# Ordering the first loads of a hand-scheduled attention + MLP kernel, with a new table of priorities

## The chip, the cores and the metric

The kernel runs on one core of a Trainium2 chip. The metric is device time in microseconds (us) of one execution; lower is better. The profiled execution has a "span", from its first to its last instruction, which is some 1.7 us shorter than the time of the same run. Engines: PE (TensorE, matrix products), ACT (ScalarE), DVE (VectorE), POOL (GpSimd), and SP, the engine that issues the DMAs here.

On one core, a run counts as slow when it is over 1.5% above the fastest run of the same kernel.

## The reference

One layer norm feeds two branches whose outputs are added to the input:

```python
xn  = layernorm(x)                           # x: 2048 x 512
out = x + attention(xn) + silu(xn @ w1) @ w2 # w1: 512 x 1792
# attention: 32 heads of 16, 4 segments of 512 rows; in each segment
#   local part : softmax(q k^T / 4 + causal mask) v
#   memory part: phi(q) M / (phi(q) z), with M, z summed over earlier segments
#   o = g * memory + (1 - g) * local,  g = sigmoid(beta), one gate per head
#   the result is o @ wo
```

All tensors are bf16. Two details matter. The scores cannot start before q and k exist, and the fixed order of both kernels begins with the k and q products, so wk and wq are needed first. And `beta`, 32 numbers, is needed only when local and memory parts are weighted, much later.

## The kernel before

A planner in Python runs when the kernel is built. It makes a list of operations, each with an engine, an estimated duration and dependencies, and lays them out greedily: at each step every engine picks, among its operations that could start first, the one with the lowest `due`. The result is a fixed instruction order for each engine. `due` comes from `PRIO`, a table of 1,064 numbers found by an offline search against the planner's own estimate.

```python
def op(...):                            # cut to one line
    o.due = int(PRIO[unit] if PRIO else due)

def load(keys, fn, due, lat, nb=0):     # a DMA issue on SP; lat: estimated time to landing
    return op("SP", 520, lat, fn, due, w=keys, kind="load", not_before=nb)

load([("x", 0, 0)], ld_x(0, 0), 0, 2300)        # operation 0
load([("x", 0, 1)], ld_x(0, 1), 1, 2900)        # 1
load([("wk",)], ld_w("wk", "A_wk"), 2, 4200)    # 2
load([("wq",)], ld_w("wq", "A_wq"), 3, 5000)    # 3
load([("wv",)], ld_w("wv", "A_wv"), 4, 6900)    # 4
load([("w1",)], ld_w("w1", "B_w1"), 5, 11500)   # 5
load([("x", 1, 0)], ld_x(1, 0), 6, 12000)       # 6
load([("x", 1, 1)], ld_x(1, 1), 7, 12500)       # 7
load([("w2",)], ld_w("w2", "B_w2"), 8, 17000)   # 8
load([("wo",)], ld_w("wo", "A_wo"), 9, 18000)   # 9
op("SP", 1600, 2300, beta, 30000, w=[("bcol",)], kind="load", not_before=14000)  # 10: three small DMAs
# ... (cut) loads of x for segments 2 and 3, not before 26000 ns
```

The estimates of landing, `lat`, rise in the order of the list, but each stays with its load wherever the load is placed. The planner doesn't know that loads share one queue. With `PRIO`, the due time written in the list is ignored, and the old table put wk seventh and wq ninth.

```python
key, _, t, o = min(
    (
        -(10**9) if o.kind == "S" else -(10**8) if o.kind == "PV" and after_s else o.due,
        o.n, t, o,
    )
    for t, o in cands if t <= tmin + {"S": SLACK_S, "exp": 200}.get(o.kind, 0)
)
```

"S" are the score products (q k^T) into `psS`, a single PSUM buffer. Each of the 80 is read by one big exponential on ACT (128 x 2048, 1.88 us), so scores and exponentials alternate. The user of `beta` is the gate, on ACT and POOL; it stands among the exponentials:

```python
def gate(K):
    for n, c, sc in ((64, 0, -0.5), (16, 1, -0.5), (P, 2, 0.5)):
        g = K.gcol[0:n, c : c + 1]
        K.nc.scalar.activation(out=g, in_=K.bcol[0:n, c : c + 1], func=AF.Tanh, scale=sc)
        K.nc.gpsimd.tensor_scalar(
            out=g, in0=g, scalar1=1.0, scalar2=0.0, op0=ALU.add, op1=ALU.add
        )
op("ACT", 700, 400, gate, 36000, r=[("bcol",)], w=[("gcol",)])
```

The softmax here doesn't subtract the row's maximum and nothing guards it: scores larger than these inputs give would overflow.

Of the kernel before, what the change touches and what calls it, by code (L numbers as in the profile page):

```python
# [16 lines left out]
S = 2048  # L17
# [17 lines left out]
SLACK_S = 140  # L35
# [47 lines left out]
class Op:  # L83
# [7 lines left out]
    -223886, -213142, 63705, 177752, 22538, 11838, 1323, -178954, 67144, 313387, 373006, -21515,  # L91
    -130461, -113893, -392237, -225704, -39247, 247190, 57588, 37283, 207192, -218991, 308507,
    -194611, -201621, 108204, 211932, 13621, 191955, -74326, -130154, -216427, 359611, -155119,
    211539, -11405, 331460, -686597, 105504, -573941, 130428, -187273, 363457, -85128, 26133,
    606903, -210234, -48374, -297013, 60798, -86752, 132802, 118851, -12546, 272870, -132982, 56639,
    276934, -30169, -123830, -33891, 174675, 348195, 23174, 311678, 85348, -120105, 131741, -343655,
    153058, 64242, -128605, 30195, 365519, 429917, 204159, 219852, 21171, 419872, 463879, -39762,
    -46133, -123987, 230528, 410142, 339477, 252091, -376123, -41682, 194296, 83947, -35832,
    -276286, 321232, -145594, -524228, -181427, -294070, 301993, 29359, -431758, -6753, -615407,
    130942, -456522, 728205, -128974, -538322, -36195, 368831, 324874, -212795, 3954, 24792, -96637,  # L100
    135035, 97677, 219505, 275780, 142732, -348149, -42889, 172395, 167352, 445291, -66175, -102014,
    -372410, 37471, 173532, 19691, -321703, -129398, 162590, 242096, 70777, 150541, -390982, -61352,
    -251857, -193457, 59903, -1614, 300474, 282740, 64973, 208882, 311930, -142375, -31593, -66521,
    -186886, 104021, 173402, -103896, -310717, 19751, 214713, 406435, 162192, -59093, 104904, 15373,
    45642, -403821, 22920, -13329, -380672, -322525, -303614, -46256, 222990, 291846, 12582, 267990,
    156615, 34382, -299125, 93507, 42449, 95428, -70203, -72443, 71244, 84531, 355865, 214206,
    -51920, -867600, 450492, 653865, -124671, 291884, 109183, 371865, 49608, -24648, 12887, -52544,
    -107952, -196109, 126671, 210183, -73712, 65341, 327031, -272143, -81544, 72729, -135801,
    -44066, 81811, 504708, 242995, 322335, -108412, -218919, -420413, -151337, -268135, -61088,
    268203, -550455, 477679, 162280, 41945, 309807, 448567, -47735, 200, 219528, 257937, 308851,  # L110
    -4743, -77883, -321233, 271147, -158470, 70467, 161654, 183567, 109398, -58824, -26320, 319089,
    493049, -52901, -178879, -318844, -4681, 117496, -14816, -838748, -2790, -229724, 28284,
    -189806, 89509, -447653, -277801, 127390, -244192, 475390, 349318, -116303, 280396, -285555,
    297487, 646605, 233173, -505163, -444113, 544129, -247005, 360900, -207069, -518091, -25000,
    323687, 213790, 324998, 112059, -81929, 274310, -115137, -12298, -189996, 159842, -413389,
    43372, -6542, -361722, -117190, -181623, -209128, -95238, 561466, 65715, -562084, -398228,
    117345, 279724, -310824, 398752, 938804, 77902, -125744, -459583, -384468, 26680, 561173,
    156446, -76157, 212032, -558595, 670013, 310578, 166237, -657264, 247523, -22846, 83566, 303142,
    -142496, 182886, 339220, 121663, -215925, 16861, 413809, 204410, 470135, 547364, -35878, 56737,
    252649, 486999, 381304, 384370, 425566, -354622, -51398, 196368, -161285, -109610, 560866,  # L120
    582723, -347380, -50235, 665289, -31010, 302067, 262506, -423589, -284834, -306774, 300711,
    -55492, 364398, 189503, 404079, 265748, 536775, 393349, -113863, 795645, -43828, 650707, 144536,
    868479, 516187, -336929, 318957, -92765, -338554, 352320, 422504, 56954, -123776, 108661,
    -418893, 98624, -349798, 208932, -144548, 8421, 233612, 65865, 326473, 284664, -67576, 96797,
    54991, -86892, 225526, 106850, 145126, 120193, 89893, 406763, 9214, 938427, 229693, -8110,
    616416, 103328, 601485, -144743, -67828, 740495, -200273, 291414, 748381, 56526, 92062, 345312,
    27253, -319794, 121568, 100442, 437124, 302161, 427765, 119763, 54441, 335976, 297665, 714657,
    41060, 793859, -259467, -129865, 308076, 498970, 681180, 116086, -225150, 378154, 415845,
    349221, 140566, 644683, -124115, 173680, 11971, 399022, 400290, 655824, 224582, 305365, 700076,
    625561, 187056, -525661, 616109, -2218, -22419, -99519, -92630, -166436, -392391, 93383,  # L130
    -460739, 172173, 238659, -372180, 188021, 230765, 371908, 47890, -6346, 8122, -144220, 249370,
    617233, 40145, -137502, 166780, 97040, -40096, 58727, -276233, -226357, 345646, 181978, -46103,
    772501, 365050, -148600, -36316, 267507, 127581, -38572, 142382, -52113, 575324, -222372,
    -268435, 26343, 529066, 40508, 373069, 429467, 79014, 440198, 315329, 86662, -41603, 237281,
    476327, 356731, -99018, 265712, -249558, -49914, 4028, 301058, 592205, 470876, 154418, 96955,
    485673, -2411, 14098, 13735, 316163, -318442, 413197, -129226, 109000, -116788, 219469, 153645,
    47167, 518007, 183833, -30350, 699233, 211894, 322323, 263597, 83130, -227535, 236095, -85087,
    -113604, 37411, 430015, -2870, -5612, 278579, -362276, -83264, -81427, -199134, 58995, 569470,
    -109610, 201191, -659359, -190562, -403082, 227854, 631137, 226817, 48231, 419085, 98761,
    -79066, 216112, -643907, -35621, 508726, 32353, 93064, 164762, -316492, 382792, -92758, -169368,  # L140
    455126, -39072, 6864, -316685, 131619, 348879, 834577, -178579, 74157, -506959, 182481, 63075,
    -21058, 299346, 172655, -386925, -24498, -548053, 207605, 558009, -93423, -118774, -237046,
    217183, 552102, 680873, 306408, 531969, 445316, 434638, -200823, -13485, 118730, 20688, 107964,
    112865, 757871, -432568, -10969, 19072, 150683, 254327, 496949, -352315, 24731, -389605, -3730,
    320564, 957932, 373690, -57423, 83479, 690429, -376908, 253627, -914692, -30234, 29173, 73881,
    -206246, 230654, 445275, -30519, -472093, 309832, -118161, 1178607, 215829, -9127, 648306,
    427924, 332526, -202779, -136804, 21232, 611557, -135946, -198518, -226779, 238655, 259659,
    -193804, -267942, 238993, 81582, 270060, 107098, -115249, 474096, 12986, -18534, -216434,
    150625, 374025, 342160, 549418, 222611, 495391, 828493, 146361, 96622, 298454, -480090, 158394,
    -392573, 149486, 186067, -119362, 376881, -43805, -127619, -11352, -248776, -165409, 209429,  # L150
    917995, 102430, -131646, 202189, -151133, -397805, 219744, 242953, 155680, 79047, -1170477,
    7101, -3583, -372569, 484448, -160719, -239932, -484839, 5499, 210265, 306700, 256289, -348081,
    139835, 163395, -104101, 211338, 49815, 269523, 204999, 433551, 475223, -16588, 383302, -108148,
    165310, 444383, 89977, -44060, 198590, -369426, 249196, -37350, -199335, 220214, 431056, 529697,
    312339, 733114, -486947, 332194, 49609, 161813, -175730, -107076, 781937, 10229, 298989, 241713,
    110416, -111509, 121768, 243442, -152232, 353584, -245133, 182974, 37534, -157385, 569856,
    -260196, -545047, 254985, 138018, 20910, 66379, 21009, -656458, 367115, 483729, 180777, 19163,
    63118, 192957, 16971, -1949, 656916, 237358, 13970, 54310, 627127, 376175, -1475, 286123,
    312388, 30189, -484848, 289293, 961495, -115477, -152898, 258396, 175375, -401170, 350145,
    357588, 267082, -43812, -65319, -21881, 740140, 161674, 554201, 409656, 296631, 98022, 463505,  # L160
    248165, 41143, -45415, 310094, -120290, -92558, 132597, -2791, 43260, -488909, 468646, 750003,
# [24 lines left out]
class Plan:  # L186
# [763 lines left out]
    def schedule(self):  # L950
# [12 lines left out]
        mode, after_s, pend = "F", False, 0  # L963
# [194 lines left out]
```

## Time and profile before

| quantity | before | view |
|---|---|---|
| time, first three runs | 257.59 us (255.35 to 258.34) | runs |
| span of the profiled run | 253.2 us | page |
| PE / ACT busy | 89% / 77% | page, part 1 |
| first scores / first big exponential | 24.54 / 25.20 us | timeline |
| PE busy from 24.5 to 232 us | 195 of 207.5 us | stages |

The order of the loads is read from the timeline of SP. The columns are the start in us, the duration in us, the engine's queue, the line and the operation with what it writes and reads. `w` stands for w1 at the first place and w2 at the second.

```profile
0.79 1.99 SPq L296 DMA_DIRECT2D x_all<-in_A_x_dram  x4
2.82 0.47 SPq L304 DMA_DIRECT2D w<-in_B_w_dram  x1
3.33 0.51 SPq L304 DMA_DIRECT2D wv<-in_A_wv_dram  x1
3.88 0.51 SPq L304 DMA_DIRECT2D wk<-in_A_wk_dram  x1
4.43 2.68 SPq L304 DMA_DIRECT2D w<-in_B_w_dram  x1
7.16 6.01 SPq L304 DMA_DIRECT2D wq<-in_A_wq_dram  x1
13.21 1.88 SPq L304 DMA_DIRECT2D wo<-in_A_wo_dram  x1
```

The issue of wq lasts 6.01 us against about 0.5 for the first ones. I read this as the queue in front of it being full; no view shows the queue itself. What the late loads do to the PE is in its timeline; the bracket gives the idle time before an instruction and what ended it.

```profile
14.23 0.61 PE L276 MATMUL psb__201<-xnT__88,wk 128*128 128x512 bf16 x1 [4.47 <-DMA wk<-in_A_wk_dram]
...
21.01 1.89 PE L276 MATMUL psb__202<-xnT__88,wq 128*128 128x512 bf16 x4 [4.90 <-DMA wq<-in_A_wq_dram]
...
24.54 0.61 PE L609 MATMUL psS<-qT__102,kTo__96 32*128 32x512 bf16 x4
```

The first k product waits for wk until 14.23 us and the first q product for wq until 21.01 us. The layer norm had been done at 10.5 us (last cast into xnT, DVE timeline). The chain of waits that ended last, in order of time (start, duration, what), says the same for the whole execution:

```profile
4.43 2.68 SPq L304
...
7.16 13.81 DMA wq<-in_A_wq_dram
...
21.01 1.89 PE psb__202 L276 x4
```

The view by stages gives for each stretch its length and the busy time of each engine with the number of instructions, then the granted PE clock (1.00 is full), the DMA share and GB/s:

```profile
core 0: us, PE busy (x) PEld busy (x) DVE busy (x) ACT busy (x) POOL busy (x), PEclk, DMA share, GB/s
...
10.50:24.50 14.00, 5.16 (x11) 1.47 (x12) 1.38 (x2) 0.63 (x1) 1.27 (x2) 0.55 0.87 278
24.50:45.00 20.50, 18.80 (x119) 7.19 (x124) 17.92 (x36) 17.76 (x20) 16.75 (x40) 0.98 0.28 65
```

In the 14 us before the scores begin the PE works 5.16 us, at about half its clock. After that it is dense.

### The profile page before, as it was taken

The numbers are of one execution on the slowest core, as the hardware profiler recorded it, in microseconds if no ns is written. First come the engines' busy times: TensorE is split into PE (matmuls) and PEld (weight loads), VectorE is DVE, ScalarE is ACT, GpSimd is POOL, SyncE is SP. The second block draws the span as 40 slices with busy tenths as digits, with TensorE's granted clock in tenths as the row PEclk, the third lists the DMA queues.
The fourth block names the chain that finished last, engine by engine and source line by source line (L and its number), as shares of the span: only waits on it lengthen the run. The fifth ranks groups of instructions, "written<-read, shape, count | busy, mean of one in ns | idle before, by whom it ended". The sixth has DMA issues, their size and how long they took to land.

```text
span 253.2 us, 5054 instructions
## 1 busy us (share of the span) xinstructions
PE 224.4 (89%) x1887; PEld 96.9 (38%) x1920; DVE 178.2 (70%) x308; ACT 194.5 (77%) x170; POOL 130.0 (51%) x231
## 2 busy tenths in 40 slices
PE   7226997989999899999999998897999999997994
PEld 7102332443344343353443433342343434343441
DVE  4612988988758997688747799868676896366532
ACT  2100997998999989999899898997989887996000
POOL 4420996776769743358752447694833443432000
PEclk9955999999999999999999999999999999999999
DMA  6994125210322103214210221220101202201202
GB/s 204 385 349 142 22 41 146 25 31 14 63 52 45 23 18 121 64 43 108 51 34 10 86 71 31 68 66 12 56 22 54 70 14 89 73 4 36 76 22 83
DMA packets 29344, 18.52 MB, mean 73 GB/s; under 512 B 15752, under 2 KB 28808, under 8 KB 29320
## 3 DMA queue, kind: packets, MB, share of 16 engines
q1 hardware_dynamic: 29176, 18.07, 25.1%
q8 instruction: 15, 0.25, 0.5%
q10 hardware_dynamic: 144, 0.13, 0.2%
q14 instruction: 9, 0.07, 0.1%
HBM read 11.53 MB, written 2.33 MB: 55 GB/s over the span
## 4 chain that ended last, share of the span: by engine, by line
PE 38%; ACT 16%; DVE 16%; POOL 9%; DMA 9%; issue 6%; SPq 3%; DVEq 0%; ACTq 0%; POOLq 0%
PE psb__201 L276 6%; PE psb__204 L276 6%; PE psb__202 L276 6%; DMA wq<-in_A_wq_dram 5%; PE psb__203 L276 5%; PE psS L609 5%; ACT Pt__133 L620 2%; ACT Pt__129 L620 2%; ACT Pt__131 L620 2%; PE psO__2920 L929 2%; PE psO__2921 L929 2%; PE psO__2918 L929 2%; PE psO__2919 L929 2%; SPq L304 2%; ACT Pt__130 L620 2%
## 5 line engine op out<-in xcount | busy, mean ns | idle before, releaser
L276 PEld LDWEIGHTS <-w 128*128 128x128 bf16 x224 | 20.4, 98 | 26.3 <-issue 6.6
L620 ACT ACTIVATE Pt__128<-psS 128x2048 bf16<-128x2048 f32 x10 | 18.8, 1879 | 9.2 <-PE psS L609 8.7
L620 ACT ACTIVATE Pt__129<-psS 128x2048 bf16<-128x2048 f32 x10 | 18.8, 1878 | 2.9 <-PE psS L609 2.6
L620 ACT ACTIVATE Pt__130<-psS 128x2048 bf16<-128x2048 f32 x10 | 18.8, 1877 | 1.8 <-PE psS L609 1.5
L620 ACT ACTIVATE Pt__132<-psS 128x2048 bf16<-128x2048 f32 x10 | 18.8, 1878 | 1.8 <-PE psS L609 1.6
L620 ACT ACTIVATE Pt__135<-psS 128x2048 bf16<-128x2048 f32 x10 | 18.8, 1876 | 1.5 <-PE psS L609 1.2
L620 ACT ACTIVATE Pt__133<-psS 128x2048 bf16<-128x2048 f32 x10 | 18.8, 1878 | 1.5 <-PE psS L609 1.2
L620 ACT ACTIVATE Pt__134<-psS 128x2048 bf16<-128x2048 f32 x10 | 18.8, 1878 | 1.5 <-PE psS L609 1.3
L620 ACT ACTIVATE Pt__131<-psS 128x2048 bf16<-128x2048 f32 x10 | 18.8, 1879 | 1.0 <-PE psS L609 0.8
L634 POOL TENSOR_SCALAR_AFFINE_SELECT Pt__134<-Pt__134 128x512 bf16<-128x512 bf16 (+1 forms) x14 | 10.4, 756 | 10.0 <-ACT Pt__134 L620 9.9
L634 POOL TENSOR_SCALAR_AFFINE_SELECT Pt__133<-Pt__133 128x512 bf16<-128x512 bf16 (+1 forms) x15 | 10.2, 695 | 9.0 <-ACT Pt__133 L620 9.0
L634 POOL TENSOR_SCALAR_AFFINE_SELECT Pt__130<-Pt__130 128x512 bf16<-128x512 bf16 (+1 forms) x14 | 10.1, 738 | 9.1 <-ACT Pt__130 L620 9.1
L634 POOL TENSOR_SCALAR_AFFINE_SELECT Pt__135<-Pt__135 128x512 bf16<-128x512 bf16 (+1 forms) x14 | 9.2, 671 | 10.7 <-ACT Pt__135 L620 10.7
L634 POOL TENSOR_SCALAR_AFFINE_SELECT Pt__129<-Pt__129 128x512 bf16<-128x512 bf16 (+1 forms) x14 | 9.7, 707 | 9.3 <-ACT Pt__129 L620 9.3
L634 POOL TENSOR_SCALAR_AFFINE_SELECT Pt__128<-Pt__128 128x512 bf16<-128x512 bf16 (+1 forms) x14 | 10.2, 740 | 8.3 <-ACT Pt__128 L620 8.3
L634 POOL TENSOR_SCALAR_AFFINE_SELECT Pt__131<-Pt__131 128x512 bf16<-128x512 bf16 (+1 forms) x14 | 10.2, 742 | 7.5 <-ACT Pt__131 L620 7.5
L634 POOL TENSOR_SCALAR_AFFINE_SELECT Pt__132<-Pt__132 128x512 bf16<-128x512 bf16 (+1 forms) x13 | 10.1, 791 | 6.9 <-ACT Pt__132 L620 6.7
L276 PE MATMUL psb__201<-xnT__89,w 128*128 128x512 bf16 x44 | 11.7, 380 | 0.1
L276 PEld LDWEIGHTS <-wk 128*128 128x128 bf16 x64 | 6.3, 103 | 12.9 <-DMA wk<-in_A_wk_dram 4.6
L276 PE MATMUL psb__203<-xnT__88,w 128*128 128x512 bf16 x32 | 8.9, 379 | 2.5 <-DVE hT__140 L570 1.5
L276 PEld LDWEIGHTS <-wq 128*128 128x128 bf16 x64 | 5.8, 100 | 13.1 <-DMA wq<-in_A_wq_dram 5.8
L938 ACT ACTIVATE x_all<-psO__2919 128x512 bf16<-128x512 f32 x1 | 0.6, 597 | 12.5 <-PE psO__2919 L929 12.5
(663 smaller groups left out, 667.9 us busy)
## 6 DMA issues: line engine op xcount, KB each, us to landing
w<-in_B_w_dram SPq DMA_DIRECT2D x2, 1792.0 KB
x_all<-in_A_x_dram SPq DMA_DIRECT2D x8, 256.0 KB
out_dram<-x_all SPq DMA_DIRECT2D x15, 128.0 KB
wv<-in_A_wv_dram SPq DMA_DIRECT2D x1, 512.0 KB
wk<-in_A_wk_dram SPq DMA_DIRECT2D x1, 512.0 KB
wq<-in_A_wq_dram SPq DMA_DIRECT2D x1, 512.0 KB
wo<-in_A_wo_dram SPq DMA_DIRECT2D x1, 512.0 KB
mrep__176<-dmem__198 SPq DMA_DIRECT2D x2, 128.0 KB
```

Of the source, the lines that this page charges most:

```text
L276: K.nc.tensor.matmul(K.bank(t)[:, 0:ncol], lhsT=lhsT(K, i), rhs=rhs(K, i), start=(i == 0), stop=(i == n - 1),)
L304: K.nc.sync.dma_start(out=getattr(K, name)[:], in_=getattr(K, src).rearrange("(ko ki) n -> ki ko n", ki=P))
L609: K.nc.tensor.matmul(K.psS[:, g, c : c + nq], lhsT=kk[r0:r1, kt * P : (kt + 1) * P], rhs=K.qT[b][r0:r1, kt * P : L], start=True, stop=True ...
L620: K.nc.scalar.activation(out=K.Pt[n % RING["Pt"]][:], in_=K.psS[:], func=AF.Exp, scale=SCALE)
L634: K.nc.gpsimd.affine_select(out=a, in_=a, compare_op=ALU.is_ge, fill=0.0, base=0, pattern=[[0, a.shape[1]], [1, P]], channel_multiplier=-1,)
L929: K.nc.tensor.matmul(K.psO[j][:, :], lhsT=a(K), rhs=b(K), start=(i == 0), stop=(i == len(seq) - 1))
L938: K.nc.scalar.activation(out=K.x_all[:, t_ % XT, :], in_=K.psO[j][:, :], func=AF.Copy, scale=0.5)
```

## The change

The intent: issue the initial loads in the order of the list, ahead of anything else on SP, so that the planner's landing times belong to the order really issued; then search the table again under that rule. No arithmetic changes. The last hunk makes a load's key its place in the list, far below every other key.

```diff
-SLACK_S = 140
+SLACK_S = 160
 ...
 PRIO = [
-    -223886, -213142, 63705, 177752, 22538, 11838, 1323, -178954, 67144, 313387, 373006, -21515,
 ... (all 1,064 numbers differ)
+    -305865, -316180, 96303, 462936, 71666, 311926, -499264, -784288, -274909, 280448, 695226,
 ...
-                        -(10**9) if o.kind == "S" else -(10**8) if o.kind == "PV" and after_s else o.due,
+                        o.n - 2 * 10**9 if o.kind == "load" else -(10**9) if o.kind == "S" else -(10**8) if o.kind == "PV" and after_s else o.due,
```

So the change has two parts: the order of the loads, and a new static order of everything else.

## The prediction

> **What bounds the kernel now.** Two parts. (1) The start. In the timeline of the DMA-issuing queue the order of loads is x (four issues), w1, wv, wk, w2, wq, wo; the old table put wk after w1 and wq after w2. The chain of waits shows a DMA wait of 13.81 us for wq. The tensor engine has its normalised input at 10.5 us (last cast into xnT in the vector timeline), but the first k product waits for wk until 14.2 (4.5 us idle) and the first q product for wq until 21.0 (4.9 us). First scores: 24.54; first big exponential: 25.20. By stages, PE is busy 5.2 of 14.0 us from 10.5 to 24.5, at a granted clock of 0.55. (2) Afterwards the tensor engine is 94% busy (195 of 207.5 us from 24.5 to 232) with ScalarE close behind (192 us, 92%); a tail of 21 us follows.
>
> **What the change does.** No arithmetic is added or removed. Loads go out as x0, x0, wk, wq, wv, w1, x1, x1, w2, wo, later ones (beta, x2, x3) before anything else ready. The rest of the static order is searched anew for that order of loads.
>
> **Costs.** The loads move at about 350 GB/s (between the landings of wk and wq 2.36 MB came in 6.8 us). The Trainium skill, "DMA: Bandwidth & Descriptors", section "Queues, rings and completion order", says descriptors are consumed in ring order on each DMA engine; the trace agrees (wq behind w2). From the first x at 3.58 us I estimate wk at 5.8, wq 7.3, wv 8.8, w1 14, x1 15.6, w2 21, wo 22.5 us. So layer norm, not DMA, then decides the start: first k product 10.5, first scores about 13.5, first exponential about 14, i.e. 11 us earlier. The PE should stay near full clock there.
>
> **How much is critical.** Nearly all: after the start PE and ScalarE are dense until 232 us. From 10.5 us about 216 us of PE work at full clock, 12.7 us of idle as now, and 3.5 us after the last product give a span of 242.7.
>
> **What is given back.** beta is issued behind wo, which the full queue lets go only at about 15 us (as now), and lands behind w2 and wo at 23 to 24. Its consumer on ScalarE (the gate) has a higher priority than before and may stand in the fixed order at about 18 us: ScalarE, hence scores and PE, would then stall up to 5 us. The s=1 transposes share that queue. I take 3 us for this, and nothing for a better table.
>
> **Prediction.** Span about 246, time 248 us (before 257.59; span plus 1.7 when profiled), 243 to 252.5 in 8 of 10. Faster by over 2%: 0.82; within 2%: 0.16; slower: 0.02.
>
> **What would show it.** Chain of waits: no wait for wk or wq, beginning with x and layer norm. Timeline: first scores 13 to 14.5; PE between 10.5 and 24.5 over 10 us busy, clock over 0.9. The later stages keep their PE density (93 to 97%). If the beta stall is real, ScalarE idles before the gate's Tanh (L375) until about 23; if not, the span comes nearer 243.
>
> **What would make it wrong.** A longer stall at beta; another late transfer (w1, x1 or its transposes); the new table having been fitted to a model that the chip doesn't follow in the middle, so that PE density there falls by over 3%.

## The result, and the profile after

| | before | after |
|---|---|---|
| time, median of 4 runs | 256.48 us | 247.01 us (246.15 to 247.35) |
| span of the profiled run | 253.2 us | 245.0 us |
| first scores / first big exponential | 24.54 / 25.20 us | 15.46 / 15.91 us |
| mean granted clock, profiled run | 0.973 | 0.984 |

The ratio is 0.9619 (95% interval 0.9543 to 0.9694), so the change is faster. Ratios are the mean time of one kernel's fast runs over that of the other's of the same rounds, so they are not quite the ratio of the medians quoted. The prediction of 248.0 us (243.0 to 252.5) holds.

The timeline of SP after the change:

```profile
1.79 0.47 SPq L307 DMA_DIRECT2D wk<-in_A_wk_dram  x1
2.31 0.51 SPq L307 DMA_DIRECT2D wq<-in_A_wq_dram  x1
2.85 0.51 SPq L307 DMA_DIRECT2D wv<-in_A_wv_dram  x1
...
7.93 8.88 SPq L307 DMA_DIRECT2D wo<-in_A_wo_dram  x1
16.96 2.82 SPq L497 DMA_TRANSPOSE phiK<-phiKT__109  x1
19.84 2.17 SPq L327 DMA_DIRECT2D bcol<-in_A_beta_dram  x3
```

wk and wq go out at 1.79 and 2.31 us. beta (`bcol`) goes out at 19.84, behind wo, whose issue now lasts 8.88 us, and behind a transpose. The PE:

```profile
11.09 1.22 PE L279 MATMUL psb__201<-xnT__88,wk 128*128 128x512 bf16 x3 [0.89 <-DVE xnT__88 L455]
12.11 1.91 PE L279 MATMUL psb__202<-xnT__88,wq 128*128 128x512 bf16 x4
...
15.46 0.39 PE L612 MATMUL psS<-qT__102,kTo__96 32*128 32x512 bf16 x4
...
28.31 0.29 PE L612 MATMUL psS<-qT__102,kTo__96 32*128 32x256 bf16 x4 [3.03 <-ACT Pt__131 L623]
...
29.73 1.91 PE L279 MATMUL psb__203<-wv,xnT__88 128*128 128x512 bf16 x4
```

No product waits for a weight; the first waits for the last cast of the layer norm. But there are two blemishes. At 28.31 us the scores had waited 3.03 us for ACT. And a group of four k or q products takes 1.91 us at 12.11 (and one of wv at 29.73), where 1.03 is normal. The stages of after, same columns as above:

```profile
10.50:24.50 14.00, 13.30 (x69) 5.00 (x72) 9.54 (x20) 7.26 (x7) 7.61 (x21) 0.88 1.09 316
24.50:45.00 20.50, 16.45 (x132) 6.90 (x133) 16.40 (x33) 16.89 (x18) 16.39 (x33) 0.92 0.37 67
```

From 10.5 to 24.5 us the PE works 13.30 us instead of 5.16. From 24.5 to 45 it works 16.45 instead of 18.80. ACT shows why:

```profile
20.66 1.88 ACT L623 ACTIVATE Pt__130<-psS 128x2048 bf16<-128x2048 f32 x1
24.72 0.20 ACT L378 ACTIVATE gcol<-bcol 64x1 f32<-64x1 bf16 x1 [2.18 <-DMA bcol<-in_A_beta_dram]
25.10 0.20 ACT L378 ACTIVATE gcol<-bcol 16x1 f32<-16x1 bf16 x1 [0.17 <-DMA bcol<-in_A_beta_dram]
26.29 0.20 ACT L378 ACTIVATE gcol<-bcol 128x1 f32<-128x1 bf16 x1 [0.99 <-DMA bcol<-in_A_beta_dram]
26.40 1.86 ACT L623 ACTIVATE Pt__131<-psS 128x2048 bf16<-128x2048 f32 x1
```

The gate's three Tanh (L378) wait 2.18, 0.17 and 0.99 us for beta's three pieces, and the exponential behind them starts only at 26.40. The chain of waits begins with x and layer norm instead of wq, and then has beta in it:

```profile
0.79 2.90 DMA x_all<-in_A_x_dram
...
9.75 1.21 DVE xnT__88 L455 x2
...
21.43 4.84 DMA bcol<-in_A_beta_dram
```

The granted clock in the same stretch, by stages again:

```profile
27.00:28.00 1.00, 0.00 (x0) 0.00 (x0) 0.00 (x0) 1.00 (x1) 0.92 (x3) 1.00 0.00 0
28.00:29.00 1.00, 0.69 (x10) 0.35 (x10) 0.76 (x2) 1.00 (x3) 1.00 (x3) 0.93 0.00 0
29.00:32.00 3.00, 3.00 (x9) 1.08 (x8) 2.30 (x6) 2.55 (x3) 2.84 (x7) 0.50 0.22 44
32.00:33.00 1.00, 1.00 (x8) 0.22 (x6) 0.98 (x3) 0.08 (x1) 0.92 (x3) 0.86 0.00 0
33.00:34.00 1.00, 1.00 (x8) 0.40 (x5) 0.58 (x1) 1.00 (x2) 1.00 (x3) 1.00 0.00 0
```

So after the 3 us gap the PE ran at half clock. From the shares of 28 to 29 and 32 to 33 us (0.93 and 0.86, a mixture of 1.00 and 0.50) I work out that the half clock lasted from about 28.9 to 32.3 us, 3.4 us. By the same reckoning from a finer view, a stretch of the same length and depth lies at 11.8 to 15.2 us, over the first k and q products.

**Where the time went.** In every kernel of the table below 24.2 us (to within 0.1) lie between the start of the last big exponential and the end. So the start of the n-th exponential, read from ACT's timeline, tells how far ahead a kernel is at each point:

| n-th big exponential starts at (us) | before | after | b_loads | a_oldloads | a_gate_late | a_gate_pad | b_loads_gate |
|---|---|---|---|---|---|---|---|
| 1st | 25.20 | 15.91 | 15.63 | 25.59 | 15.78 | 14.15 | 15.57 |
| 6th | 37.97 | 33.41 | 32.04 | 38.65 | 28.49 | 26.86 | 28.19 |
| 21st | 78.23 | 72.24 | 70.53 | 78.79 | 68.25 | 66.45 | 68.23 |
| 26th | 92.48 | 84.82 | 84.79 | 91.54 | 80.92 | 79.06 | 82.48 |
| 46th | 142.45 | 134.49 | 134.83 | 141.21 | 130.59 | 129.20 | 132.38 |
| 51st | 155.07 | 146.93 | 147.46 | 153.66 | 143.03 | 142.84 | 145.00 |
| 80th | 228.96 | 220.76 | 221.35 | 227.86 | 216.86 | 216.83 | 218.90 |

The last five columns are experiments. After is 9.3 us ahead of before at the first exponential, only 4.6 at the sixth, and 8.2 at the last. So about half of the early gain is lost within five exponentials, and 3.6 us come back later, 2.2 of them at the seventh, where before itself is held up (4.57 us from its sixth start to its seventh, 2.37 in after).

### The profile page after: what moved, and what is told of

Read it like the earlier page. It is cut to its first block, busy times and chain, and to the rows that moved or that the text cites. A ratio compares the mean times of both kernels' runs of the same rounds, so it can differ in the third digit from the quotient of the medians.

```text
span 245.0 us, 5048 instructions
## 1 busy us (share of the span) xinstructions
PE 225.1 (92%) x1887; PEld 97.3 (40%) x1920; DVE 178.7 (73%) x308; ACT 194.2 (79%) x170; POOL 129.7 (53%) x231
## 4 chain that ended last, share of the span: by engine, by line
PE 56%; DVE 14%; ACT 10%; DMA 7%; issue 5%; POOL 5%; SPq 1%; DVEq 0%; ACTq 0%; POOLq 0%
PE psb__202 L279 11%; PE psb__201 L279 9%; PE psb__204 L279 8%; PE psb__203 L279 8%; PE psS L612 7%; POOL rstd L425 2%; DMA bcol<-in_A_beta_dram 2%; PE psO__2921 L932 2%; PE psO__2920 L932 2%; PE psO__2918 L932 2%; PE psO__2919 L932 2%; DMA xnT__89<-xn__87 2%; PE psb__203 L650 2%; ACT Pt__129 L623 2%; ACT Pt__134 L623 2%
## 5 line engine op out<-in xcount | busy, mean ns | idle before, releaser
L425 POOL TENSOR_TENSOR rstd<-rstd,lnc 128x1 f32<-128x1 f32 x16 | 9.4, 589 | 1.3
```

What stands on the lines that cost most here:

```text
L425: K.nc.gpsimd.tensor_tensor(out=rs, in0=rs, in1=K.lnc[:, 1:2], op=ALU.pow)
```

## The experiments

Theory: (1) the late wk and wq cost before some 9 us, which nothing later could absorb; (2) the new table gives little by itself; (3) the wait for beta gives some microseconds back. Rivals: the table earns the gain and the load order hardly matters; or slack later in the order absorbs the stall at beta. A third way was not tried: to let the PE do products with w1 or wv, which go out ahead of wk in before, until wk has come.

All edits but one reorder the finished list `self.order` directly behind the planner's sort. So nothing is planned anew and each run differs from its base in the named place only. All results were correct. The nine kernels ran in three batches, each batch on its own chip beside its own runs of the kernel before; across batches, compare ratios rather than times.

### b_loads: only the order of the loads, with the old table

```diff
         self.order.sort(key=lambda o: (o.start, o.n))
+        at = [i for i, o in enumerate(self.order) if o.n < 10]
+        for i, n in zip(at, range(10)):
+            self.order[i] = self.ops[n]
```

> The kernel before with its static order on PE, ACT, DVE and POOL untouched; only the ten initial loads are put into the new order. Theory (the late wk and wq are the cost): first k product at about 11, first scores at 15 to 16 instead of 24.54 us, the chain of waits no longer holds wk or wq. The gate stands after the third big exponential in this order too (31.9 us before, so about 22.7 now) and beta lands at about 24, so some 2 us are lost there: time 247 to 250 against about 256.5. Rival (the new table earns the gain, the loads' order hardly matters because later slack absorbs a late start): 254 or more.

Measured on the PE:

```profile
15.18 0.39 PE L609 MATMUL psS<-qT__102,kTo__96 32*128 32x512 bf16 x4
```

First scores at 15.18 us, no wait for wk or wq, and waits of 2.4 us of ACT for beta. Median 251.12 us (247.3 to 253.12), ratio 0.9719 (0.9642 to 0.9795). Two of its four runs count as slow (252.14 and 253.12, at clocks of 0.973 and 0.980), so the ratio rests on the other two, 247.3 and 250.09. The mechanism came as the theory says and the rival falls. The median lies above the 247 to 250 expected; why this kernel scatters by 2.4% is open.

### a_oldloads: the new table, with the old order of the loads

```diff
         self.order.sort(key=lambda o: (o.start, o.n))
+        at = [i for i, o in enumerate(self.order) if o.n < 10]
+        for i, n in zip(at, (0, 1, 7, 6, 5, 4, 2, 8, 3, 9)):
+            self.order[i] = self.ops[n]
```

> The kernel after with its new order on all compute engines, but the ten initial loads in the old order. Theory: first scores back at 24 to 25 us; the wait at beta disappears, because the gate then comes after beta has landed; so 9 us lost and 3 to 5 won back: 250 to 254. Rival (the table earns it): 246 to 249.

Measured on the PE:

```profile
15.06 0.61 PE L279 MATMUL psb__201<-xnT__88,wk 128*128 128x512 bf16 x1 [4.99 <-DMA wk<-in_A_wk_dram]
...
21.82 1.89 PE L279 MATMUL psb__202<-xnT__88,wq 128*128 128x512 bf16 x4 [4.87 <-DMA wq<-in_A_wq_dram]
```

First scores at 25.15 us; 0.6 us left of the wait for beta. Median 254.22 us, ratio 0.9942 (0.9888 to 0.9996), by the 2% line the same as before. The median lies just above the 250 to 254 expected, far from the rival's 246 to 249. Without the loads' order the table is worth 0.6%.

### b_wq_only: before, with wq and w2 swapped

```diff
         self.order.sort(key=lambda o: (o.start, o.n))
+        at = [i for i, o in enumerate(self.order) if o.n < 10]
+        for i, n in zip(at, (0, 1, 7, 6, 5, 4, 2, 3, 8, 9)):
+            self.order[i] = self.ops[n]
```

> The kernel before with only wq and w2 swapped among the loads (x, w1, wv, wk, wq, w2, wo). If loads land in the order of issue at about 350 GB/s, wk still lands at 14.2 and wq at about 15.7 instead of 21.0. First scores at 18.5 to 19.5, 5 to 6 us earlier; time 250 to 252.5. Rival (landing times are not set by the bytes ahead in the queue): wq stays near 20 and the time at 255 or more.

Measured on the PE:

```profile
15.31 0.61 PE L276 MATMUL psb__201<-xnT__88,wk 128*128 128x512 bf16 x1 [5.49 <-DMA wk<-in_A_wk_dram]
...
16.99 1.91 PE L276 MATMUL psb__202<-xnT__88,wq 128*128 128x512 bf16 x4
...
20.01 0.40 PE L609 MATMUL psS<-qT__102,kTo__96 32*128 32x512 bf16 x4
```

wk came at 15.3 us, 1.1 us later than in before, and wq did not hold the PE at all. Most of the 1.1 us need not be due to the swap: in a_oldloads, whose loads go out in the same order as in before, wk (15.06) and wq (21.82) came 0.8 us later too. First scores at 20.01, 4.5 us earlier than in before (18.5 to 19.5 was expected). Median 253.13 us, ratio 0.9814 (0.973 to 0.9898): the size fits the 4.5 us, but with two runs counted slow and an interval that crosses the 2% line the time is unclear, and the median misses the range. What the run does show is that half of the early gain comes from taking wq out from behind w2's 1.8 MB.

### a_gate_late: after, with the user of beta moved back

```diff
         self.order.sort(key=lambda o: (o.start, o.n))
+        g = self.acc[("gcol",)][1][0]
+        self.order.remove(g)
+        self.order.insert(self.order.index([o for o in self.order if o.kind == "exp"][11]) + 1, g)
```

> The kernel after with the gate (Tanh on ScalarE and its adds on POOL) moved behind the twelfth big exponential in the static order; beta's load stays where it is. Theory (waiting for beta stalls ScalarE, then POOL and the tensor engine for 3 us, and the tensor clock then drops to half for some 4 us): no wait on bcol, no 3.0 us gap of the PE before the fourth group of scores, granted clock 1.00 between 25 and 36; 242 to 244.5 against 247. Rival (slack later in the order absorbs the stall): 246 to 247.5.

Measured: median 240.97 us (240.69 to 243.11), ratio 0.944 (0.9395 to 0.9484), faster than expected. On ACT the fourth and fifth exponentials now follow without the gap:

```profile
20.54 1.88 ACT L623 ACTIVATE Pt__130<-psS 128x2048 bf16<-128x2048 f32 x1
22.94 1.88 ACT L623 ACTIVATE Pt__131<-psS 128x2048 bf16<-128x2048 f32 x1 [0.52 <-PE psS L612]
...
25.71 1.88 ACT L623 ACTIVATE Pt__132<-psS 128x2048 bf16<-128x2048 f32 x1
```

and the granted clock from 24.5 to 36 us is 1.00 (0.85 in after). In the table of exponentials the two kernels are 0.1 us apart at the first. At the fifth after is 3.45 us behind (29.16 against 25.71, the wait itself), at the sixth 4.92 (the half clock on top), at the last 3.9. So later slack absorbs only 1.0 us of the stall. The rival falls. With the interval of its ratio below that of after (0.9543 to 0.9694), this kernel beats both before and after.

The ratios make the stall cost 4.6 us (0.9619 less 0.944, times before's 256.5), but part of this is the clock elsewhere: the mean clock of after is 0.984 to 0.986 in all four runs, and in four of the six runs here it is 0.999 or 1.0, so that these lack the half clock of the start as well, which the gate's place cannot explain. The profiled run has it (0.993), so its 3.9 us is the better figure.

### a_beta_early: after, with beta's loads moved forward

```diff
         self.order.sort(key=lambda o: (o.start, o.n))
+        b = self.ops[10]
+        self.order.remove(b)
+        self.order.insert(self.order.index(self.ops[5]) + 1, b)
```

> The kernel after with beta's three small loads issued right behind w1 instead of behind wo; every compute engine keeps its order. Theory (the stall is the lateness of beta's bytes, queued behind w2 and wo): beta lands by about 16 us, the gate at 22.5 to 23 no longer waits, the PE gap of 3.0 us and the half clock after it are gone, and the time is that of a_gate_late within 0.7%: 240 to 243. Rival (the place of the gate on ScalarE costs, or beta's tiny pieces hold up x1 and w2 behind them by as much): 245 or more.

Measured: median 241.94 us, ratio 0.9455 (0.9413 to 0.9498). The gate runs at 22.3 us, in its old place, without a wait. So its place costs nothing when beta is there in time. The theory's wording was partly wrong, though. In after the bytes of the loads had mostly landed by 23 us (stage view: 67 GB/s from 23 to 24, 0 from 24 to 25), while beta landed at 24.7 to 26.3. For the most part it was late because it was issued late, at 19.84 us: SP was held in the issue of wo until 16.81, and then in a transpose's until 19.78. The planner's own plan of after (the planner run without the chip) has beta issued at about 15.2 us and landed at 19.1, against 19.84 and 26.27 measured. So about 4.7 of these 7.2 us are late issue and 2.5 slow landing. From the start of its issue beta's last piece took 6.4 us in after, but 4.6 in b_wq_only and 5.0 in a_oldloads, where it went out after nearly all of the weights had landed; by that comparison the queue in front of it cost 1.4 to 1.9 us.

### b_loads_gate: both repairs, with the old table

The two edits of b_loads and a_gate_late together on before.

> The kernel before with the new order of the initial loads and its gate moved behind the twelfth big exponential; the old table otherwise. Theory: the stall at beta costs this order as well (2.3 us of PE and about 2 us of half clock in b_loads), so 3 to 5 us under b_loads: 243 to 247. What it then lacks against a_gate_late (241) is what the new table gives by itself, apart from loads and beta: 2 to 5 us. Rival (the table gives nothing): 240.5 to 242.

Measured: median 244.93 us (242.55 to 245.96), ratio 0.9561 (0.951 to 0.9612), as expected. Against a_gate_late (0.944) the two ratios differ by 1.2% of before's 256 us, about 3 us; the profiled spans (243.1 and 241.1), both at a mean clock of 0.993, differ by 2.0. The ratios differ by more because four of the six runs of a_gate_late have a clock of 0.999 or 1.0, while five of the six here have 0.993. So about 2 us are the part of the new table alone; whether the better clock is the table's too is open. In the table of exponentials 1.6 us of it appear between the 21st and the 26th; I found no single wait that accounts for them.

### a_gate_pad: can the half clock at the start be avoided?

The edit in short; the gate is moved back as in a_gate_late:

```diff
+        # throwaway 128-column products of the identity into psS, which is free then:
+        # 12 behind the warm-up, 22 behind the second and 14 behind the fourth transposition
```

> a_gate_late with 48 throwaway products on the PE (12 behind the warm-up, 22 behind the second and 14 behind the fourth transposition, written to the scores' PSUM, which is free then), so that PE idles less between 6.6 and 11.1 us. Theory (the clock falls to 0.5 at about 12 us because the PE was little busy in the 4 us before): granted clock near 1.00 from 10.5 to 16, the first k and q groups take 0.9 instead of 1.6 to 1.7 us, first scores 1.0 to 1.7 us earlier (13.6 to 14.4), time 239 to 240.5 against 241.0. Rival (the clock falls for another reason, or the scores wait for something else): no change, 241.

Measured: the start came as the theory says.

```profile
11.02 1.02 PE L279 MATMUL psb__201<-xnT__88,wk 128*128 128x512 bf16 x4
11.88 1.03 PE L279 MATMUL psb__202<-xnT__88,wq 128*128 128x512 bf16 x4
...
13.70 0.39 PE L612 MATMUL psS<-qT__102,kTo__96 32*128 32x512 bf16 x4
```

The groups take 1.02 and 1.03 us, the granted clock is 1.00 from 6 to 16 us, and the first exponential starts at 14.15 us, 1.6 earlier than in a_gate_late. But the time is not shorter: median 241.63 us, ratio 0.9439 (0.9404 to 0.9475) against 0.944. In this profile the lead is kept until the 46th exponential and gone at the 51st. The stages there:

```profile
140.00:142.00 2.00, 0.41 (x2) 0.00 (x0) 1.97 (x5) 1.53 (x2) 1.92 (x5) 1.00 0.03 8
142.00:144.00 2.00, 1.80 (x8) 0.60 (x9) 2.00 (x5) 1.16 (x1) 1.27 (x2) 0.58 0.00 0
144.00:146.00 2.00, 2.00 (x6) 0.53 (x5) 1.62 (x3) 1.24 (x2) 0.61 (x1) 0.56 0.33 67
```

After two short waits of the PE (0.82 and 0.97 us, for DVE) the clock fell to about half for some 3.4 us. a_gate_late has the second of these waits at about the same place, without the first and without the fall. That the number of such stretches differs from run to run of one kernel is told by the timed runs: one stretch of 3.4 us at half clock lowers the mean clock by 3.4 x 0.5 / 241 = 0.007, and of the six runs of a_gate_late four have a mean clock of 0.999 or 1.0 (240.69 to 241.06 us) and two have 0.991 and 0.993 (243.11 and 242.77). A start without the half clock was thus common already, and there was little for the padding to save: 1.6 us in two of six runs, an estimate of 0.5 us on average, is below what these intervals can show.

### g_wk_later: is there slack in front of the weights?

The edit of a_gate_late, and the loads in the order x x x x wv wk wq w1 w2 wo.

> a_gate_late with the second x pair and wv put ahead of wk and wq (1.05 MB more in front of wk). Theory (layer norm, done at 11.0 us, decides the first product, not the loads): at 350 to 360 GB/s wk lands at about 8.8 and wq at about 10.2 us, still before they are needed at 11.1 and 12.1, so no DMA wait for wk or wq, first scores at 15.3 (13.7 where the clock doesn't fall), time as a_gate_late, 240.7 to 243. Rival (the start follows the weights even here): first scores about 3 us later and 243.5 or more.

Measured: no wait for a weight, first product at 11.12 us, first scores at 15.49; median 242.38 us, ratio 0.9431 (0.9377 to 0.9485). With 1.05 MB more in front of wk nothing moved. The layer norm sets the start now, in this order of loads as in that of after.

### b_rule: the rule without the new table

```diff
-                        -(10**9) if o.kind == "S" else ...
+                        o.n - 2 * 10**9 if o.kind == "load" else -(10**9) if o.kind == "S" else ...
```

This one lets the planner lay everything out anew, with the old table.

> The kernel before with the diff's last hunk alone: the rule that loads go first, so the planner lays the whole order out anew with the old table. Theory: the table's numbers were fitted to one order, and with other arrival times the order of all engines changes far down; first scores at 15 to 16, but PE density afterwards falls below the 94% of before: 248 to 260, slower than b_loads or equal. Rival (the table is robust): as b_loads, 247 to 251.

Measured: median 312.02 us, ratio 1.2178 (1.2125 to 1.223): far outside the range. The start is right (first scores 16.15 us), but no big exponential starts between 38.88 and 83.71 us. The PE does other products first and then starves beside ACT (columns of the stage view as above):

```profile
34.00:88.00 54.00, 50.84 (x288) 22.69 (x284) 39.77 (x71) 29.52 (x42) 17.12 (x30) 0.97 0.19 37
88.00:135.00 47.00, 29.25 (x320) 12.07 (x319) 25.27 (x44) 38.36 (x28) 28.18 (x40) 0.82 0.19 41
```

From 34 to 88 us the PE is busy for 50.84 of 54 us while ACT works 29.52; from 88 to 135 the PE has 29.25 us of work in 47. Which numbers of the table sent it there I did not trace. So this order of loads must not be planned with the old table; other arrival times were not tried.

### The two parts side by side

Ratios to before:

| | old table | new table |
|---|---|---|
| loads in the old order | 1 | 0.9942 |
| loads in the new order | 0.9719 | 0.9619 |
| loads in the new order, gate moved back | 0.9561 | 0.9440 |

By differences of these ratios, in per cent of before's time, the loads' order is worth 2.8 with the old table and 3.2 with the new, the table 0.6 to 1.2, the stall at beta 1.6 to 1.8. The six figures come from several batches, 0.9719 rests on two runs, and the runs differ in their clock. By the spans of the profiled runs, taken in the same pairs, the three are 7.1 to 7.6 us, 0.6 to 2.0 us and 2.5 to 3.9 us.

## Why the prediction was right

- **What bounded before: right.** The loads' order alone brings the first scores to 15.18 us (b_loads), and undoing it alone brings them back to 25.15 (a_oldloads).
- **The loads move at about 350 GB/s in order of issue, so layer norm decides the start: right.** after waits for no weight, and g_wk_later shows slack of over 1 MB. By the stage view of after the DMA moved 316 to 426 GB/s in each microsecond from 6 to 18, 366 on average. The landing times themselves were estimates and were not seen, since nothing waited; where wk was waited for, it came at 14.2, 15.1 and 15.3 us (before, a_oldloads, b_wq_only) behind the same loads, a scatter that is unexplained.
- **"First scores 13 to 14.5", an 11 us gain, "clock over 0.9": too good.** The first scores came at 15.46 and the first exponential 9.3 us earlier. The layer norm finished 0.5 us later than in before (10.95 us; with the new order and the old loads, in a_oldloads, 0.3 later), and the step that failed was "The PE should stay near full clock there": 0.88 from 10.5 to 24.5 us, with half clock at 11.8 to 15.2. a_gate_pad, with full clock, has its first scores at 13.70 and its first exponential at 14.15, the "about 14" of the prediction. So this one term, the clock at the start, was worth 1.6 us.
- **beta: right in mechanism, small in size.** "I take 3 us for this"; the exponentials measure 3.9 us at the end, and the ratios (0.9619 against 0.944) 1.8% or 4.6 us, the clock of the start included (see a_gate_late). The wait itself was sized well, 3.45 us at the fifth exponential. The term left out was the half clock after the gap, 1.5 us at the sixth exponential. The reason for beta's lateness was partly wrong, see a_beta_early.
- **"Nothing for a better table": wrong in size.** It gives about 2 us (b_loads_gate against a_gate_late, profiled spans), less where the stall at beta or the late loads stand in front of it (0.6 and 1.1 us).
- **Nearly all on the critical path: right.** What is won at the first exponential is still there at the last: from before to a_gate_late 9.4 us at the first, 12.1 at the last, where most of the surplus is the table's (with the old table, in b_loads_gate, 9.6 at the first and 10.1 at the last).

So the total is right to 1 us partly because errors cancelled: 1.7 us less at the start and 0.9 us more at beta (both by the exponentials' starts), against about 2 us from the table. That they cancelled was luck.

The Trainium skill was used twice. "DMA: Bandwidth & Descriptors", section "Queues, rings and completion order", says that each DMA engine consumes descriptors in ring order; wq came behind w2 in before, and no longer held the PE in b_wq_only, so the runs agree. "TensorE: Matmul & The Clock Gate", section "Part 1: The HAM clock gate", which the prediction should have drawn on, says that the PE's clock is halved after idle windows of about 3.4 us, that these windows run freely of the kernel, and that the effect varies from run to run. The runs agree in the length and in the variation: two stretches at 0.50 of 3.4 us each in after, and mean clocks of 0.991 to 1.0 among runs of one kernel (a_gate_late). On how much idle it takes they do not, see the last section.

## What to carry to other kernels

Let the first consumers decide the order of loads on a shared queue, and look at what stands last in it too: a tiny late load whose user stands early in a fixed order stalled ACT, POOL, PE and DVE for about 3 us each and cost about 4. When a static order is planned against estimated arrival times, the estimates must belong to the order really issued, and a table of priorities fitted to one set of arrivals has to be tested before it is reused with another (22% slower here, in the one case tried). Before counting on a gain at the start, ask whether it can be lost again to the PE's clock.

## What the Trainium skill lacked or had wrong

- "TensorE: Matmul & The Clock Gate", section "Part 1", gives one idle window of about 3.4 us as what halves the clock. Here shorter idle did it: at the start of after the clock fell at about 11.8 us with no gap of the PE over 1.41 us, later after one gap of 3.03 us, and in a_gate_pad after two waits of 0.82 and 0.97 us with work between them. Further down the page speaks of gaps of over about 3 us, and under "A second HAM failure mode" of frequent short idling, so part of this is known to it; but it has no figure for how much activity in a window suffices, and these runs do not settle it.
- "DMA: Bandwidth & Descriptors" has, as far as I found, no figure for how long an issuing engine is held behind many queued bytes: the issue of wo took 8.88 us in after and that of wq 6.01 us in before, against 0.5 us for the first issues, and everything behind it on SP waited.
